# Half slots that gather at their head, without a drain of GpSimd: fused attention and expert layers on one core

## The chip, the cores and the metric

The kernel runs on one core of a Trainium2 chip. The metric is the device time of one execution in microseconds (us). The kernel before took 798.23 us, the median of three runs (797.21 to 799.9).

## What is computed

The reference has two parts. The first is attention over 8 sequences of 448 tokens with 12 heads of 64, with a sigmoid in place of a softmax. The second sends each of the 3584 tokens (768 values) to one of 8 experts:

```python
attn = 1.0 / (1.0 + np.exp(-scores)); attn_out = np.matmul(attn, v)
logits = x @ w_gate
e_idx = np.argmax(logits, axis=1)
for e in range(E):
    mask = e_idx == e
    h = np.maximum(x[mask] @ w1[e], 0.0)
    ye = h @ w2[e]
    out[mask] = gate_w[mask, None] * eom[mask, e, None] * ye
```

All of it is float32. The tokens of an expert are known only on the chip, after the gates.

## The kernel before, in words

Attention comes first. Its rows go to a table in device memory (`x_dram`), and a list of tokens for each expert is built beside it. Then the expert layers run in slots. A slot is a group of tokens of one expert: 256 in a full slot (`slot`, L622), 192 in a wide slot (`wide_slot`, L669), 128 in a half slot (`half_slot`, L693). The number of each kind depends on the data, so `build` (L901) writes the full slots that always exist as straight code and wraps every further slot in an `If` on a count read from the chip (L970, L975, L980). With these inputs three wide slots and two half slots run; the other six half slots, like the other five wide slots, are skipped. The two half slots are the last work of the kernel.

Every product of a slot is made with operands split in a high and a low float32r part: ScalarE (ACT) makes the high part, VectorE (DVE) the low part (`split`, L534; `split_w1_row`, L548; `low_w1`, L541). TensorE (PE) multiplies the tokens by w1 (in a half slot L720 to L722), ACT applies the ReLU, PE transposes the result (`turn`, L702) and multiplies it by w2 (`layer2_mm`, L597). `layer2_out` (L613) scales the two halves of an output row on ACT (L616) and, behind the second, GpSimd (POOL) writes 128 rows to the output with one indirect DMA (L618).

A slot also prepares the next one. SP loads the next slot's weights (`load_slot`, L518; `load_w2`, L530). POOL gathers rows of `x_dram` into the one buffer `xg` with one indirect DMA for each group of 32 tokens times four parts (`gather`, L501, issued at L504): four DMAs for a half slot. DVE turns `xg` over (`turn_x`, L558, at L561), and the result is split for the next slot.

The order on each engine is the order of the program: nothing is moved by a scheduler. In a half slot j of the kernel before it is, on POOL: from the second half slot on a `drain()` of the engine (L699); after `turn_x` of half slot j + 1 the gathers for half slot j + 2 (L736), which need `xg` to be free; then the output DMA of half slot j (L618). The last wide slot gathers for two half slots ahead, so that half slot 0 finds in `xg` the tokens of half slot 1. The lists and the weight tables have entries for all eight half slots. Where a half slot does not exist, its list points to filler rows; its gathers, its `turn_x` and its splits are still issued by the slot ahead of it, and the weights of it are not transferred.

```python
if j:
    nc.gpsimd.drain()
...
self.turn_x(nx)
if j + 2 < E:
    self.gather(self.half_lists(j + 2))
```

`slot` has one more drain of POOL, in the last full slot that is written as straight code (L638). At the end of the program the framework itself issues drains on every engine and a barrier of all engines (they carry line L1016). On the path of a skipped `If` each engine makes up for the semaphore counts of the code left out; on POOL one of these is the instruction INC_SWDGE_SEM (L973 for the wide slots, L978 for the half slots).

Of the kernel before, what the change touches and what calls it, by code (L numbers as in the profile page):

```python
# [22 lines left out]
E = 8  # L23
# [31 lines left out]
def r32(ap):  # L55
    return ap.bitcast(F32)


class Kernel:
# [633 lines left out]
    def half_slot(self, j, y):  # L693
        nc = self.nc
        nx = None
        if j + 1 < E:
            nx = self.load_slot(self.tab_b, j + 1, self.half_lists(j + 1))
        if j:
            nc.gpsimd.drain()  # L699
        (wh, wl), (xh, xl), (hh, hl) = self.w1s, self.xs, self.hs  # L700

        def turn(n):  # L702
            ps = self.take("x", self.psx).rearrange("p a (b t) -> p (a b) t", b=2)
            for i in range(4):
                nc.tensor.transpose(ps[:, i], self.hb[:, 128 * (4 * n + i):128 * (4 * n + i + 1)], self.ident)
            fs = slice(4 * n, 4 * n + 4)
            self.split(ps, hh[:, fs, 0:HS], hl[:, fs, 0:HS])

        w2 = [self.w2_rows(k) for k in range(4)]
        low = lambda k: nc.vector.tensor_tensor(w2[k][2], w2[k][0], r32(w2[k][1]), ALU.subtract)  # L710
        for n in range(2):
            c = slice(512 * n, 512 * n + 512)
            ps = self.take("h", self.psh)
            for d in range(6):
                if n == 1 and d == 3:
                    turn(0)
                    low(2)
                    nc.scalar.copy(w2[3][1], w2[3][0])
                    low(3)
                nc.tensor.matmul(ps, xh[:, d, 0:HS], wh[d][:, c], start=(d == 0), stop=False)  # L720
                nc.tensor.matmul(ps, xh[:, d, 0:HS], wl[d][:, c], start=False, stop=False)
                nc.tensor.matmul(ps, xl[:, d, 0:HS], wh[d][:, c], start=False, stop=(d == 5))  # L722
            if n == 0:
                self.split_w2(0)
                self.split_w2(1)
            nc.scalar.activation(self.hb[:, c], ps, AF.Relu)
            if n == 0:
                nc.scalar.copy(w2[2][1], w2[2][0])
        cur = dict(lt=self.ltb[:, j])
        pss = [self.take("y", self.psy)[:, 0:384] for n in range(2)]  # L730
        self.layer2_mm(pss[0], 0, 0, range(2))
        turn(1)
        if nx is not None:
            self.turn_x(nx)
            if j + 2 < E:
                self.gather(self.half_lists(j + 2))  # L736
            self.split_w1(0)
            for k in range(3):
                self.split_x(nx, k)
            self.split_w1(1)  # L740
        self.layer2_mm(pss[0], 0, 0, range(2, 4))
        self.layer2_mm(pss[1], 0, 1, range(4))
        self.load_w2(nx)
        if nx is not None:
            self.split_w1_row(4)
        for n in range(2):
            self.layer2_mm(pss[n], 0, n, range(4, 8))
            self.layer2_out(pss[n], cur, 0, n, y)
        if nx is not None:
            self.split_w1_row(5)  # L750
# [269 lines left out]
```

## Time and profile before

| what | before |
|---|---|
| median of three runs | 798.23 us (797.21 to 799.9) |
| the profiled execution | 799.36 us |
| its span, first to last instruction | 797.6 us |
| PE busy | 771.8 us, 97% |
| DVE busy | 498.2 us, 62% |
| ACT busy | 490.0 us, 61% |
| POOL busy | 330.4 us, 41%, 468 instructions |
| software DMA queue (POOL's) | 10016 packets, 24.85 MB |
| hardware DMA queue (SP's) | 27696 packets, 119.56 MB |

The span is the time that the trace covers; 1.76 us of the profiled execution lie outside it. Busy times do not count sequencer instructions such as drains, branches and semaphore operations. Those appear in the views with a q behind the engine's name (POOLq). A line in such a view can be that of a helper. A row of the timeline gives the start in us, the duration in us, the engine, the line, the operation, what is written from what, and the idle time ahead of it.

### The profile page before, as it was taken

What the parts mean: (1) busy time and instruction counts of PE and PEld (TensorE: products, weight loads), DVE (VectorE), ACT (ScalarE), POOL (GpSimd) and SP (SyncE); (2) the same over time, 40 slices, a digit from 0 to 9 for tenths busy, and PEclk for the clock granted to TensorE, in tenths of its full rate; (3) what the DMA queues carried; (4) which work ended last, traced back from release to release, by engine and by line L of the source; (5) the groups of instructions that cost most, each with busy time, mean ns of one, the idle gap of its engine ahead of it and who ended that gap; (6) DMA issues with size and microseconds to landing.
All of it is one profiled execution on the core that took longest, in us unless ns stands there. A gap on an engine that the chain in (4) does not pass through costs nothing. (4 is left out here: it accounts for less than half of the span.)

```text
span 797.6 us, 15037 instructions
## 1 busy us (share of the span) xinstructions
PE 771.8 (97%) x5724; PEld 564.3 (71%) x5724; DVE 498.2 (62%) x779; ACT 490.0 (61%) x662; POOL 330.4 (41%) x468
## 2 busy tenths in 40 slices
PE   9999999999999999899999999999999998999893
PEld 4333433333333379799899999999999997888773
DVE  3344435434456668977685775857758575787685
ACT  5666666666668556465574565745657464667674
POOL 4003302320333475657836626345162551543453
PEclk9999999999999999999999999999999999999997
DMA  6353453425458350247468776521165835956861
GB/s 255 133 209 123 163 203 140 180 100 209 150 168 344 110 179 6 80 147 240 184 232 295 236 252 243 169 68 31 50 236 174 299 114 204 349 219 237 288 239 44
DMA packets 37807, 145.61 MB, mean 183 GB/s; under 512 B 5703, under 2 KB 7919, under 8 KB 33744
## 3 DMA queue, kind: packets, MB, share of 16 engines
q1 hardware_dynamic: 27696, 119.56, 42.3%
q0 software_dynamic: 10016, 24.85, 9.4%
q8 instruction: 51, 0.84, 0.4%
q14 instruction: 44, 0.36, 0.2%
HBM read 153.00 MB, written 23.05 MB: 221 GB/s over the span
## 5 line engine op out<-in xcount | busy, mean ns | idle before, releaser
L579 PE MATMUL ps<-rounded 128*128 128x512 f32 (+1 forms) x672 | 229.3, 390 | 5.1 <-ACTq L968 2.9
L504 POOL DMA_INDIRECT plain<-x_dram,lxs x122 | 170.5, 1398 | 151.0 <-DVE plain L561 109.4
L782 ACT ACTIVATE a<-ps,bias_s 128x896 f32<-128x896 f32 x168 | 169.0, 1007 | 101.7 <-PE ps L780 95.2
L580 PE MATMUL ps<-rounded 128*128 128x256 f32 (+1 forms) x672 | 185.3, 276 | 0.9 <-DVE rounded L542 0.9
L536 DVE TENSOR_TENSOR w2l<-plain,w2h 128x1536 fp32r<-128x1536 f32 x60 | 105.3, 1757 | 96.3 <-ACT w2h L535 63.8
L780 PE MATMUL ps<-kqv 64*64 64x448 f32 x1344 | 159.3, 540 | 1.4 <-issue 0.6
L789 PE MATMUL ps<-a,kqv 64*64 64x448 f32 x1344 | 157.4, 536 | 0.0
L579 PEld LDWEIGHTS ps<-rounded 128*128 128x128 f32 x672 | 127.5, 190 | 29.5 <-ACTq L968 3.2
L604 PE MATMUL ps<-w2h,h 128*128 128x384 f32 x432 | 144.8, 335 | 0.0
L606 PE MATMUL ps<-w2h,h 128*128 128x384 f32 x432 | 144.4, 334 | 0.0
L605 PE MATMUL ps<-w2l,h 128*128 128x384 f32 x432 | 144.3, 334 | 0.0
L580 PEld LDWEIGHTS ps<-rounded 128*128 128x128 f32 x672 | 128.9, 192 | 1.2 <-DVE rounded L542 1.2
L542 DVE TENSOR_TENSOR rounded<-plain,rounded 128x2048 fp32r<-128x2048 f32 x46 | 103.7, 2285 | 6.2 <-ACT rounded L539 4.6
L789 PEld LDWEIGHTS ps<-a,kqv 64*64 64x64 f32 x1344 | 52.3, 133 | 74.5 <-issue 73.3
L780 PEld LDWEIGHTS ps<-kqv 64*64 64x64 f32 x1344 | 49.1, 133 | 75.8 <-issue 63.5
L535 ACT CAST w2h<-plain 128x1536 fp32r<-128x1536 f32 x60 | 88.1, 1472 | 10.6 <-PE ps L819 4.4
L539 ACT CAST rounded<-plain 128x2048 fp32r<-128x2048 f32 x46 | 87.5, 1902 | 0.0
L587 ACT COPY gl<-ps 128x256 f32<-128x256 f32 (+1 forms) x112 | 40.2, 359 | 70.2 <-PE ps L580 59.7
L604 PEld LDWEIGHTS ps<-w2h,h 128*128 128x128 f32 x432 | 81.1, 188 | 2.3 <-issue 1.8
L605 PEld LDWEIGHTS ps<-w2l,h 128*128 128x128 f32 x432 | 81.1, 188 | 0.1
L606 PEld LDWEIGHTS ps<-w2h,h 128*128 128x128 f32 x432 | 81.1, 188 | 0.0
L616 ACT ACTIVATE y<-ps,lts 128x384 f32<-128x384 f32 x50 | 29.0, 580 | 69.3 <-PE ps L606 49.6
(206 smaller groups left out, 691.4 us busy)
## 6 DMA issues: line engine op xcount, KB each, us to landing
plain<-w SPq DMA_DIRECT2D x68, 768.0 KB
plain<-w SPq DMA_DIRECT2D x48, 1024.0 KB
kqv<-kqv SPq DMA_DIRECT2D x23, 1344.0 KB
x_dram<-xt SPq DMA_DIRECT2D x8, 1344.0 KB
plain<-w SPq DMA_DIRECT2D x6, 512.0 KB
plain<-x_dram,lxs POOLq DMA_INDIRECT x122
kqv<-kqv SPq DMA_DIRECT2D x1, 896.0 KB
lst<-plain POOLq DMA_DIRECT2D x1, 726.0 KB
```

Of the source, the lines that this page charges most:

```text
L504: self.nc.gpsimd.indirect_dma_start(out=s["xg"][:, g], out_offset=None, in_=x4, in_offset=bass.IndirectOffsetOnAxis(ap=s["lx"][:, g:g + 1] ...
L535: self.nc.scalar.copy(hi, raw)
L536: self.nc.vector.tensor_tensor(lo, raw, r32(hi), ALU.subtract)
L542: self.nc.vector.tensor_tensor(self.w1p[1][k], self.w1r[:, 2 * k:2 * k + 2], r32(self.w1p[0][k]), ALU.subtract)
L579: nc.tensor.matmul(out, wh[d][:, c], both, start=(d == 0), stop=False)
L580: nc.tensor.matmul(ps[:, 0:n], wl[d][:, c], self.xc[:, d, 0, 0:n], start=False, stop=(d == 5))
L604: nc.tensor.matmul(ps, hh[:, f, tk], wh, start=(f == 0), stop=False)
L605: nc.tensor.matmul(ps, hh[:, f, tk], wl, start=False, stop=False)
L606: nc.tensor.matmul(ps, hl[:, f, tk], wh, start=False, stop=(f == 7))
L780: nc.tensor.matmul(ps[half[h], j, 0:S], kg[half[j], e, 0, o:o + 64], kg[half[j], e, 1], start=True, stop=True)
L782: nc.scalar.activation(at[u % 4], ps[:, :, 0:S], AF.Sigmoid, bias=self.bias_s, scale=1.0 / math.sqrt(D))
L789: nc.tensor.matmul(self.ps_o[e][h][half[j], 0:S], v[half[h], 6 if i == 3 else 3 * e + c, j], a[half[h], j], start=(i in ((0, 3 if h else 4 ...
```

## The change

From the second half slot on, a half slot issues the gathers for the next half slot as its first work on POOL. The gathers behind `turn_x` are gone, and so is the drain. Half slot 0 gathers nothing.

```diff
         if j + 1 < E:
             nx = self.load_slot(self.tab_b, j + 1, self.half_lists(j + 1))
-        if j:
-            nc.gpsimd.drain()
+        if nx is not None and j:
+            self.gather(self.half_lists(j + 1))
         (wh, wl), (xh, xl), (hh, hl) = self.w1s, self.xs, self.hs
...
         turn(1)
         if nx is not None:
             self.turn_x(nx)
-            if j + 2 < E:
-                self.gather(self.half_lists(j + 2))
             self.split_w1(0)
             for k in range(3):
                 self.split_x(nx, k)
```

## Rows read from the trace of the kernel before

**Rows 1.** Chain that ended last, from 785 us on: start us, us, what.
```profile
790.91 0.95 POOL plain L504
```

**Rows 2.** Timeline of POOL, half slots 0 and 1.
```profile
767.04 2.91 POOL L504 DMA_INDIRECT plain<-x_dram,gl  x1 [0.30 <-issue]
...
772.49 1.36 POOL L504 DMA_INDIRECT plain<-x_dram,gl  x1 [0.30 <-issue]
774.15 1.41 POOL L618 DMA_INDIRECT out<-y,gl  x1 [0.30 <-issue]
785.34 1.76 POOL L504 DMA_INDIRECT plain<-x_dram,gl  x1 [9.77 <-issue]
...
792.16 1.00 POOL L618 DMA_INDIRECT out<-y,gl  x1 [0.30 <-issue]
```

**Rows 3.** Timeline of ACT, the last output scalings of half slots 0 and 1.
```profile
767.48 1.03 ACT L616 ACTIVATE y<-ps,gl 128x384 f32<-128x384 f32 x2
...
785.56 0.58 ACT L616 ACTIVATE y<-ps,gl 128x384 f32<-128x384 f32 x1 [0.33 <-PE ps L606]
```

**Rows 4.** Drains of POOL by line: durations in ns (min/median/max), first and last start.
```profile
L638 POOLq DRAIN  x1: 7182/7182/7182, 411.8 to 411.8; - x1
...
L699 POOLq DRAIN  x1: 15910/15910/15910, 768.6 to 768.6; - x1
...
L1016 POOLq DRAIN  x1: 537/537/537, 796.3 to 796.3; - x1
...
L1016 POOLq DRAIN  x1: 109/109/109, 797.0 to 797.0; - x1
```

**Rows 5.** Stretches: us, PE, PEld, DVE, ACT, POOL busy (xinstructions), PEclk, DMA share, GB/s.
```profile
411.90:775.70 363.80, 356.82 (x2079) 328.70 (x2078) 255.16 (x318) 225.87 (x329) 162.00 (x109) 1.00 0.58 203
775.70:797.60 21.90, 9.83 (x57) 9.32 (x55) 12.83 (x12) 9.79 (x12) 6.60 (x5) 0.77 0.19 58
...
776.00:777.50 1.50, 1.50 (x10) 1.37 (x9) 1.50 (x2) 1.32 (x2) 0.00 (x0) 1.00 0.67 261
777.50:784.50 7.00, 7.00 (x44) 6.99 (x43) 7.00 (x9) 5.93 (x7) 0.00 (x0) 1.00 0.02 5
```

**Rows 6.** DMA issues on POOL's queue, 0 to 411.9 us.
```profile
lst<-plain POOLq DMA_DIRECT2D x1, 726.0 KB
plain<-x_dram,lxs POOLq DMA_INDIRECT x40
lst<-meta,posi POOLq DMA_INDIRECT x32
...
out<-y,lts POOLq DMA_INDIRECT x6
hb<-lst,gl POOLq DMA_INDIRECT x5
wg<-wgo POOLq DMA_DIRECT2D x1, 48.0 KB
...
lists<-lst,gl POOLq DMA_INDIRECT x2
```

**Rows 7.** Timeline of DVE, half slots 0 and 1.
```profile
766.80 2.29 DVE L542 TENSOR_TENSOR rounded<-plain,rounded 128x2048 fp32r<-128x2048 f32 x1
...
771.27 3.42 DVE L536 TENSOR_TENSOR w2l<-plain,w2h 128x1536 fp32r<-128x1536 f32 x2
...
779.91 0.97 DVE L561 STREAM_TRANSPOSE plain<-plain 128x768 f32<-128x768 f32 x1
...
786.18 2.35 DVE L536 TENSOR_TENSOR rounded<-plain,rounded 128x1024 fp32r<-128x1024 f32 x2
```

**Rows 8.** POOL's sequencer where the skipped slots end: durations in ns, first and last start.
```profile
L973 POOLq INC_SWDGE_SEM  x1: 2253/2253/2253, 760.1 to 760.1; - x1
...
L978 POOLq EVENT_SEMAPHORE  x4: 17/43/43, 795.2 to 795.5; - x4
...
L978 POOLq INC_SWDGE_SEM  x1: 278/278/278, 795.6 to 795.6; - x1
```

## The prediction

> **What bounds the kernel now.** I read the chain of waits first, then POOL's timeline, then the rows of the drains. TensorE is busy for 97% of the span, but not at the end. The chain that ended last runs in its last stretch through POOL alone: it passes through a gather at 790.91 us [rows 1] that fetches filler rows for a half slot that does not exist. The output of half slot 1 was ready long before: ACT finished the scaling at 785.56 + 0.58 = 786.14 us [rows 3], but the output DMA, last in POOL's order, was issued from 792.16 to 793.16 us [rows 2]. In front of it stood four gathers, the first from 785.34 us, and in front of those the drain of L699. That drain was reached at 768.6 us and took 15.91 us, until 784.5 us [rows 4]; POOL's last instruction ahead of it, the output DMA of half slot 0, ended at 774.15 + 1.41 = 775.56 us [rows 2]. So for 8.95 us the drain alone kept POOL. Behind the last output DMA come its landing (POOL's sequencer goes on at 795.2 us, 2.04 us after the issue [rows 8]), the make-up of semaphores, the drains of the program's end and a barrier, up to 797.6 us.
>
> What does a drain wait for? Not for data: the 392 KB of the output DMA of half slot 0 (261 GB/s over 1.5 us) are through by 777.5 us, and from there to 784.5 us the DMA engines carry 5 GB/s [rows 5], with no POOL instruction. The three drains that have work behind them line up with something else, the number of DMAs that POOL has issued since the drain before. Up to the drain of L638 these are 40 + 32 + 6 + 5 + 2 + 1 + 1 = 87 [rows 6], and it takes 7.18 us [rows 4]: 82.5 ns each. Between it and L699 every POOL instruction is a DMA, 109 of them [rows 5], and the drain takes 8.95 us after the last: 82.1 ns each. From there to the end there are five [rows 5], and the first drain of the program's end takes 0.537 us, against 0.109 us for the one after it with none left [rows 4]: 86 ns each. I read this as bookkeeping of the ring, some 82 ns for each DMA that has not been accounted for, done when a drain asks for it.
>
> **The change, part by part.**
>
> *The gathers behind turn_x and at the head.* In half slot 0 four gathers go, so its output DMA no longer stands behind them. Its scaling ends at 767.48 + 1.03 = 768.51 us [rows 3]. A POOL DMA that meets a DVE subtraction of two SBUF tensors ends about 0.87 us after that subtraction: the gather of 767.04 ended at 769.95 us and DVE's operation at 769.09 us; the gather of 772.49 ended at 773.85 us and the first of DVE's pair at 771.27 + 1.71 = 772.98 us [rows 2, 7]. So the output DMA ends at about 769.96 us. Half slot 1's four gathers follow at once; `xg` is free, since half slot 0's turn_x lies ahead of all this. They take the places that the trace has from 769.95 to 772.2, 772.49 to 773.85 and 774.15 to 775.5 us, and one from 775.85 us, that ends at 776.9 us if it meets no DVE operation and at 778.6 us if it meets a whole one of 1.71 us. The output DMA's data were down by 1.94 us after its issue ended [rows 5], with four times a gather's bytes; at most that much more makes 780.5 us for the last gather.
>
> *Who waits for them now.* DVE's turn_x in half slot 1 started at 779.91 us [rows 7], so it may come 0 to 0.6 us later. Behind it on DVE and ACT stand splits for a slot that does not exist, and the last scaling; ACT idled 0.33 us ahead of that one [rows 3]. I take 0 and keep +0.3 us. PE waits for none of it: turn_x comes after the last operand of half slot 1. SP's queue carries no weights then.
>
> *The last output DMA.* Nothing stands in front of it any more: drain and gathers are gone, POOL is free from 778.6 us at the latest. It is ready at 786.14 us and meets DVE's pair of 786.18 us, 2.35 us for two [rows 7]: the first ends at 787.36, the DMA at 788.2 us. If it met neither it would end at 787.2, if both at 789.4 us. Against 793.16 us this is **-5.0 us** (-6.0 to -3.8).
>
> *The drain.* L699 is taken away with its 8.95 us of work, which stood ahead of gathers that nobody used; that gain is inside the -5.0 us and not counted again. But the 109 DMAs that it accounted for are still there when the program's end drains POOL, with the last output DMA 110 (four gathers fewer in half slot 0, four as before in half slot 1, counting from L638). At 82.2 ns that drain takes 9.0 us instead of 0.54 us: **+8.5 us**. Nothing covers it: in the trace it begins at 796.3 us, 1.1 us after the landing, with all other engines done, and the barrier waits for it. If the work starts only after landing, 109 DMAs take 784.5 - 777.5 = 7.0 us, and the term is +6.5 us. If a drain's time does not depend on what is outstanding, it is 0. I take +8.5 us, since three drains of 5, 87 and 109 DMAs lie on one line through it.
>
> *The make-up of semaphores.* INC_SWDGE_SEM on the skipped path took 2.25 us at 760.1 us and 0.28 us at 795.6 us [rows 8]. The first stood behind some hundred DMAs not yet drained, the second behind five; but the first was also the first of its kind and ran under weight loads. If the ring is the reason, this one costs 2.0 us more now. I take 0, from the row at the same place, and keep +2.0 us.
>
> **Sum:** -5.0 + 8.5 + 0 + 0 = +3.5 us. The profiled execution (799.36 us for a span of 797.6) would become 802.9 us; it stood 1.1 us above the median of 798.23 us, so the forecast for the median is 801.8 us, 0.4% slower. With all ends of the terms it runs from -6.0 + 6.5 = +0.5 to -3.8 + 0.3 + 8.5 + 2.0 = +7.0 us: 798.7 to 805.2 us. About 0.3%, or 2.4 us, is what a measurement of this kernel can tell from no change.
>
> **The rivals.**
>
> *The drain's time does not come back (faster).* The mechanism is in the last drain of the program: if it stays near 0.54 us, only the -5.0 us is left: 793.2 us. For it speaks that a drain written by the kernel need not do the same as the one of the framework; against it, that the latter took five times the 0.109 us of its successor with just five DMAs to account for [rows 4]. It decides from the point where the last drain is under 0.54 + 5.0 = 5.5 us. The Trainium skill, in "VectorE: DVE Perf Modes", section "The DRAIN you can't avoid", says that the drains of a program's preamble and postamble are about 12 ns on all five engines, constant: by that rule this rival wins, with 793.2 us. POOL's 537 and 109 ns do not agree with it.
>
> *Half of it comes back (no change).* POOL is idle from about 778.6 to 786.1 us, and if a part of the bookkeeping is done there without being asked, or while the last DMA lands, some 4.3 us remain: -0.7 us, 797.5 us. Against it: between the two drains POOL was busy for only 162 of 363.8 us [rows 5], and L699 still shows 82 ns for each of 109.
>
> *The gathers land late (slower still).* Turn_x then holds the last scaling, one for one beyond 0.33 us. With quiet queues from 768 us on there is little to make them late; a delay of 5 us beside the forecast would give 806.8 us.
>
> **How the numbers follow.** The forecast has 0.74, the faster rival 0.15, the half 0.07, late gathers 0.04. The ends of the terms leave some 0.10 of the forecast's chance under +2.4 us. So: slower by over 0.3% 0.64 + 0.04 = 0.68; within 0.3% 0.10 + 0.06 = 0.16; faster 0.15 + 0.01 = 0.16. The range takes the forecast and the half, from 797.5 to 805.5 us, and leaves out the faster rival and late gathers, about 0.2. The likeliest case's own range is 798.7 to 805.2 us.
>
> **What would show it.** In the changed kernel's profile the output DMA of half slot 0 should be issued at about 769 us and four gathers right behind it; turn_x of half slot 1 should start at 779.9 to 780.5 us; the last output DMA should end at about 788.2 us, and POOL's sequencer pass L978 at about 790.3 us. Then the first drain of the program's end should take about 9 us instead of 0.54 us and be the last item of the chain. If that drain is short, the forecast is wrong and the faster rival holds; if INC_SWDGE_SEM shows 2 us, the sum was 2 us too low; if turn_x starts after 781 us, the gathers were late.

## The result, and the profile after

The changed kernel took 806.56 us (median of four runs, 806.43 to 808.18) against 798.03 us (with a fourth run of the kernel before): a ratio of 1.0108, 95% interval 1.0086 to 1.013. It is slower by 8.5 us, where 3.5 us had been forecast, and it lies 1.1 us above the range. The profiled execution took 808.18 us with a span of 806.5 us.

POOL's timeline in the two half slots (start us, us, engine, line, operation, idle time ahead) answers to [rows 2]:

```profile
771.78 1.14 POOL L618 DMA_INDIRECT out<-y,gl  x1 [15.43 <-ACT y L616]
773.23 1.98 POOL L504 DMA_INDIRECT plain<-x_dram,gl  x1 [0.30 <-DVE rounded L536]
...
778.81 0.95 POOL L504 DMA_INDIRECT plain<-x_dram,gl  x1 [0.30 <-issue]
789.37 1.86 POOL L618 DMA_INDIRECT out<-y,gl  x1 [9.61 <-ACT y L616]
```

The four gathers follow the output DMA of half slot 0 at once, and the last output DMA waits for nothing but ACT's scaling. These rows of DVE and ACT, half slot 1, answer to [rows 3, 7]:

```profile
782.87 0.97 DVE L561 STREAM_TRANSPOSE plain<-plain 128x768 f32<-128x768 f32 x1
...
788.51 0.58 ACT L616 ACTIVATE y<-ps,gl 128x384 f32<-128x384 f32 x1 [0.32 <-PE ps L606]
```

Turn_x does not wait for the gathers. But the scaling ends at 789.09 us, 2.95 us later than before: all of this stretch, both half slots, is late. Measured from the end of the scaling, the last output DMA ends after 2.14 us (791.23 us) against 7.02 us before. That is the gain, 4.9 us. What follows it is lost again. These are the sequencer rows of POOL where skipped code ends (L966 the full slots, L971 the wide, L976 the half slots) and at the end of the program, to be read against [rows 4, 8]; durations in ns:

```profile
L966 POOLq INC_SWDGE_SEM  x1: 1790/1790/1790, 675.4 to 675.4; - x1
...
L971 POOLq INC_SWDGE_SEM  x1: 2253/2253/2253, 763.1 to 763.1; - x1
...
L976 POOLq INC_SWDGE_SEM  x1: 2373/2373/2373, 793.7 to 793.7; - x1
...
L1014 POOLq DRAIN  x1: 9039/9039/9039, 796.3 to 796.3; - x1
```

The last drain takes 9.04 us in place of 0.54 us, and INC_SWDGE_SEM 2.37 us in place of 0.28 us. With the same landing time (2.47 against 2.44 us from the end of the issue to INC_SWDGE_SEM) the end of the program changes by -4.9 + 2.1 + 8.5 = +5.7 us. The other 2.9 us arose far ahead of the half slots. 0.6 us of them are there before 30 us (a copy of DVE to `xh` starts at 29.95 us against 29.34 us). The routing's reciprocal at L299, still attention, stands at 277.46 us against 275.15 us, 2.3 us late. Stretches of the changed kernel (us, then PE, PEld, DVE, ACT, POOL busy, PEclk, DMA share, GB/s):

```profile
262.00:266.00 4.00, 2.80 (x9) 0.61 (x10) 2.25 (x4) 1.01 (x1) 3.26 (x11) 1.00 0.27 80
266.00:268.00 2.00, 1.51 (x9) 0.92 (x12) 1.17 (x2) 1.01 (x1) 0.91 (x7) 0.65 0.00 0
268.00:270.00 2.00, 2.00 (x16) 1.26 (x12) 0.22 (x2) 1.01 (x1) 0.00 (x0) 0.50 0.00 0
```

and of the kernel before:

```profile
262.00:266.00 4.00, 2.75 (x14) 0.63 (x11) 1.67 (x3) 1.01 (x1) 3.52 (x14) 1.00 0.27 74
266.00:268.00 2.00, 2.00 (x23) 1.40 (x26) 1.53 (x3) 1.90 (x2) 0.32 (x2) 1.00 0.00 0
268.00:270.00 2.00, 2.00 (x22) 0.96 (x17) 1.12 (x4) 1.03 (x2) 0.00 (x0) 1.00 0.33 35
```

In both, PE is idle for some 1.2 of the 4 us from 262 to 266 us; in the changed kernel TensorE's granted clock then fell to 0.50 (1.2 GHz) until 270 us, in the kernel before it stayed at 1.00 (2.4 GHz). A second such stretch lies at the head of the first wide slot. Its rows, that of the kernel before ahead of the changed one's:

```profile
661.30:664.70 3.40, 3.40 (x13) 3.40 (x14) 1.40 (x1) 1.49 (x2) 0.54 (x1) 0.50 0.96 303
662.50:669.40 6.90, 6.24 (x23) 6.24 (x24) 2.11 (x2) 1.80 (x2) 1.33 (x2) 0.51 0.90 317
```

Here both kernels ran at the lower clock, the changed one twice as long. ACT's cast at 650.50 us is 2.2 us late, its copy at 675.86 us 3.3 us. So the lateness of this execution grew by 1.7 us at the first fall of the clock and by 1.1 us at the second; by the half slots a little of it was made up again. Whether the change has a part in this was a question for the runs.

### The profile page after: what moved, and what is told of

Read it like the earlier page. It is cut to its first block, busy times and chain, and to the rows that moved or that the text cites. A ratio compares the mean times of both kernels' runs of the same rounds, so it can differ in the third digit from the quotient of the medians.

```text
span 806.5 us, 15030 instructions
## 1 busy us (share of the span) xinstructions
PE 775.1 (96%) x5724; PEld 566.5 (70%) x5724; DVE 498.3 (62%) x779; ACT 491.0 (61%) x662; POOL 327.6 (41%) x464
## 3 DMA queue, kind: packets, MB, share of 16 engines
q0 software_dynamic: 9824, 24.46, 9.0%
## 5 line engine op out<-in xcount | busy, mean ns | idle before, releaser
L504 POOL DMA_INDIRECT plain<-x_dram,lxs x122 | 172.3, 1412 | 142.9 <-DVE plain L561 99.1
```

The lines of the kernel that those rows point to most:

```text
L504: self.nc.gpsimd.indirect_dma_start(out=s["xg"][:, g], out_offset=None, in_=x4, in_offset=bass.IndirectOffsetOnAxis(ap=s["lx"][:, g:g + 1] ...
```

## The experiments

The runs came from several chips; the kernel before took 794 to 800 us on them, so each is given as a ratio to the kernel before on its own chip. The times are medians; a ratio is estimated from all runs and can differ a little from the quotient of the two medians. "Number 114" is the 114th DMA that POOL issued since the drain of L638, and "accounts" is my word for the bookkeeping of DMAs that a drain has yet to do.

### The drain behind the gathers

```diff
         if nx is not None and j:
             self.gather(self.half_lists(j + 1))
+            nc.gpsimd.drain()
```

> The changed kernel with the drain put back into half slot 1, behind the four gathers instead of ahead of them. Theory (a drain, and INC_SWDGE_SEM too, pays for every DMA that POOL issued since the last drain): the drain begins when the fourth gather is issued, takes 109 x 82 ns = 8.9 us, and is over just before the last scaling is ready, so it costs nothing. The first drain of the program's end then has one DMA left and takes about 0.2 us, INC_SWDGE_SEM about 0.3 us. Time: the changed kernel less 8.8 less 2.1 us, 795.6 us; if the 2.8 us by which the changed kernel came late already ahead of the half slots go as well, 793 us. Rival (the last drain is long because of where it stands, or its length has nothing to do with the count): the drain in half slot 1 or the one at the end does not follow the count, the last one stays near 9 us, time 806 us. Rival for INC_SWDGE_SEM (long the first time or under weight loads, not for the count): 0.3 us cannot be told apart here, see the run with drains in the wide slots.

Measured: 789.93 us against 795.12 us, a ratio of 0.9941 (0.992 to 0.9961). The drain, the last drain and the last INC_SWDGE_SEM:

```profile
L700 POOLq DRAIN  x1: 15043/15043/15043, 766.1 to 766.1; - x1
...
L1015 POOLq DRAIN  x1: 212/212/212, 786.9 to 786.9; - x1
...
L977 POOLq INC_SWDGE_SEM  x1: 198/198/198, 786.2 to 786.2; - x1
```

The fourth gather ended at 772.19 us and the drain at 781.14 us: 8.95 us for 109 DMAs, as in the kernel before. The output DMA behind it was issued at 782.07 us, 0.5 us after the end of the scaling at 781.54 us, so the drain is covered. One line decides the sign of the change: with a drain behind them the gathers at the head are worth 0.6%, and the drain's absence costs more than that.

### Only the drain taken out

```diff
-        if j:
-            nc.gpsimd.drain()
```

> The kernel before with only the drain of half slot 1 taken out; the gathers stay behind turn_x. Theory: POOL's four gathers in half slot 1 start when turn_x is through, at about 781 us, and the last output DMA ends some 3 to 4 us earlier than the 793.2 us of before; then the last drain takes 114 x 82 ns = 9.4 us and INC_SWDGE_SEM about 2.3 us: 798.0 - 3.5 + 8.9 + 2.1 = 805.5 us, up to 808 us with the late start seen in the changed kernel. Rival (it is the gathers at the head that lengthen the end): the last drain stays at 0.5 us and the time is 794.5 us.

Measured: 793.85 us, a ratio of 0.9992 (0.9977 to 1.0007): no difference that can be told. The theory failed. The last drain came out short, as the rival has it, but the 3.5 us that both had counted on did not come: the gathers, the first at 773.78 us, kept POOL until 783.23 us. The last output DMA, POOL's INC_SWDGE_SEM and the last drain:

```profile
783.53 1.00 POOL L618 DMA_INDIRECT out<-y,gl  x1 [0.30 <-issue]
...
L976 POOLq INC_SWDGE_SEM  x1: 337/337/337, 786.9 to 786.9; - x1
...
L1014 POOLq DRAIN  x1: 703/703/703, 787.5 to 787.5; - x1
```

No drain stands between L638 and the end, 114 DMAs were issued, and yet the last drain is short. The scaling ended at 778.78 us, so the output DMA ended 5.75 us behind it, 1.3 us better than before; the two short items cost 0.2 us more. The 0.703 us are those of about seven outstanding DMAs on the scale of the other rows. So either something had cleared all but some seven of the accounts on the way, in this kernel and not in the changed one, which issues 110, or it matters where the gathers lie (the rival). The runs with more gathers test that.

### Drains in the wide slots

```diff
         self.layer2(cur, 0, 1, self.ys[0])
+        self.nc.gpsimd.drain()
```

(at the end of `wide_slot`; the half slots as changed)

> The changed kernel with a drain at the end of each wide slot, none in the half slots. Theory (both instructions go by the count): the three drains take about 85 x 82 ns = 7 us, then 8 DMAs each, 0.7 us, all while POOL has nothing else to do; INC_SWDGE_SEM behind the wide slots falls from 2.25 to about 0.3 us, so turn_x of half slot 0 starts up to 2 us earlier and PE's wait in half slot 1 shrinks; the last drain has 6 DMAs and takes 0.6 us, the last INC_SWDGE_SEM about 0.3 us. Time: 806.6 - 8.4 - 2.0 - 1.5 = 794.7 us. Rival for INC_SWDGE_SEM (first of its kind, or weight loads on the DMA engines): the one behind the wide slots stays at 2.25 us, and the time is 796.2 us.

Measured: 790.03 us, a ratio of 0.994 (0.9919 to 0.9962). The drains in the wide slots, INC_SWDGE_SEM behind the wide slots and the drains at the end:

```profile
L692 POOLq DRAIN  x3: 4490/8438/8477, 694.4 to 747.0; - x3
...
L972 POOLq INC_SWDGE_SEM  x1: 173/173/173, 756.3 to 756.3; - x1
...
L1015 POOLq DRAIN  x3: 46/109/632, 785.5 to 786.7; - x3
```

INC_SWDGE_SEM right behind a drain takes 0.17 us where it took 2.25 us, under the same weight loads: it goes by the count of undrained DMAs, as the drain does. The first of the three drains has 88 DMAs and ends 7.25 us after the last issue, as the count has it. The two later ones had eight DMAs and still took 4.5 and 8.4 us. Each stood behind an output DMA, with the weights of the next slot on the DMA engines, and these two output DMAs (issued at 723.83 and 747.26 us) landed late, 3.9 and 7.8 us after their start:

```profile
out<-y,lts POOLq DMA_INDIRECT x1, 3.9
out<-y,lts POOLq DMA_INDIRECT x1, 7.8
```

That is at 727.7 and 755.1 us; the drains ended 0.4 us later, at 728.1 and 755.5 us. Three drains of five or eight DMAs in the kernel with both kinds of drain (below) also ended 0.3 to 0.4 us after a landing. So I read a drain as lasting until the accounts are done and the last data have landed, whichever comes later. The prediction's "Not for data" holds for its three drains, whose data were down first, and not in general. No run changed the landing alone.

### Thirty small DMAs

```diff
         o = 6 * DF * 4
+        small = c(0, 30, 16, dt=F32, parts=1)
+        for i in range(30):
+            self.nc.gpsimd.dma_start(small[:, i], self.wgo[i:i + 1, 0])
```

(in `memory`; the half slots as changed)

> The changed kernel with 30 further DMAs of 64 bytes on POOL's queue, ahead of the drain of L638; the output stays the same. Theory (the count of DMAs): the drain of L638 has 117 in place of 87 and takes 117 x 82.5 ns = 9.6 us. Rival (packets or bytes): 30 to 480 packets more on 3744, 0.1% of the bytes more: 7.2 to 8.1 us. The last drain stays at 9.0 us, the time within 0.3% of the changed kernel, since nobody waits for the drain of L638.

Measured: 800.41 us in one run, beside a median of 795.12 us for the kernel before. The drain of L638 (L641 here):

```profile
L641 POOLq DRAIN  x1: 9629/9629/9629, 410.3 to 410.3; - x1
```

9.63 us for 117 DMAs against 7.18 us for 87: 30 DMAs of 64 bytes cost 2.45 us, 82 ns each, as much as a gather of 96 KB or an output DMA of 384 KB. The count is what is paid for, not packets or bytes. The small DMAs made more packets than the expectation allowed for, 960 (10784 in place of 9824 on POOL's queue), but packets do not order the drains: these 117 DMAs made 4784 of them, and the 109 of the kernel before, whose drain is shorter, 5920. The last drain stayed at 9.03 us.

### More gathers

```diff
         if nx is not None and j:
             self.gather(self.half_lists(j + 1))
+            self.gather(dict(lx=self.lxb[:, j + 1], xg=self.xg[:, 4:8]), groups=range(4))
```

> The changed kernel with four further gathers of filler rows in half slot 1, into a part of the buffer that nobody reads. They stand behind the four gathers, while POOL has nothing else to do. Counted from the drain of L638 the last output DMA is number 114 in place of 110. In the kernel before without its drain, number 114 came and the last drain took 0.70 us with no drain ahead of it. Theory (the ring has room for the rows of fewer than 114 such DMAs, and when it is full the accounts are cleared on the way at no visible cost): the last drain takes 0.7 us, INC_SWDGE_SEM 0.34 us, and more work makes the kernel 8.3 + 2.0 us faster than the changed kernel, some 0.6% faster than the kernel before. Rival (it was the gathers behind turn_x, or the four gathers in half slot 0, that kept the end short there): the last drain takes 114 x 82 ns = 9.4 us and INC_SWDGE_SEM 2.5 us, time as the changed kernel or 0.5 us more.

Measured: 790.84 us against 793.96 us, a ratio of 0.9962 (0.9946 to 0.9977): four useless gathers make the changed kernel faster than the kernel before.

```profile
776.84 2.11 POOL L504 DMA_INDIRECT plain<-x_dram,gl  x1 [0.30 <-issue]
782.96 1.51 POOL L618 DMA_INDIRECT out<-y,gl  x1 [4.01 <-ACT rounded L535]
...
L977 POOLq INC_SWDGE_SEM  x1: 338/338/338, 786.9 to 786.9; - x1
...
L1015 POOLq DRAIN  x1: 703/703/703, 787.4 to 787.4; - x1
```

The last drain has the same 0.703 us as in the kernel with the drain taken out, whose gathers lie elsewhere. So the rival, the place of the gathers, falls. The output DMA, number 114, started 1.7 us after its scaling ended at 781.22 us, where the changed kernel has 0.3 us; if this is the clearing, it costs at most 1.5 us. In the kernel with only the drain taken out no DMA near number 114 has more than the usual 0.30 us of idle time ahead of it, so nothing of the clearing is seen there.

With two further gathers (the same line with `range(2)`):

> The same with two further gathers: the last output DMA is number 112. Theory: if the ring is full only at 113 or 114, the last drain takes 112 x 81 + 130 ns = 9.2 us and INC_SWDGE_SEM 2.5 us, time as the changed kernel; if it is full at 111 or 112, the drain takes 0.5 to 0.7 us, some 10 us less. Rival (the place of the gathers): as the changed kernel in either case.

Measured: 798.42 us in one run. The last INC_SWDGE_SEM and the drains at the end:

```profile
L977 POOLq INC_SWDGE_SEM  x1: 2413/2413/2413, 783.7 to 783.7; - x1
...
L1015 POOLq DRAIN  x3: 46/109/9197, 786.6 to 796.4; - x3
```

112 DMAs are not cleared, 114 are. The threshold of these runs lies between, with DMAs of 128 rows; with 30 small ones among them 117 went by without clearing, so it is not the bare number of DMAs that decides. Where the count starts is open: the two kernels that were cleared issue 201 DMAs from the program's start, this one 199, and no run tells a count from the start from one since the last drain.

### The drain ahead of the gathers

```diff
         if nx is not None and j:
+            nc.gpsimd.drain()
             self.gather(self.half_lists(j + 1))
```

> The changed kernel with the drain put back at its old place, ahead of the gathers, which stay at the head of half slot 1. Theory (a drain holds POOL for 82 ns per DMA, and whoever needs what is queued behind it waits): it accounts for 105 DMAs, 8.6 us from the end of half slot 0's output DMA; the four gathers follow, and turn_x of half slot 1 waits for them 5 to 6 us; the last scaling and the last output DMA are late by as much; the last drain (5 DMAs) 0.5 us and INC_SWDGE_SEM 0.3 us are short again. Time within 1 us of the kernel before: what the drain's absence saves at the end is what turn_x loses. Rival (the gathers' place hardly matters, only whether there is a drain): turn_x does not wait, as in the run with the drain behind the gathers, 0.6% faster than before.

Measured: 800.39 us against 799.71 us, a ratio of 1.0013 (0.9992 to 1.0033): no difference that can be told. The drain, and turn_x of half slot 1:

```profile
L699 POOLq DRAIN  x1: 9950/9950/9950, 765.5 to 765.5; - x1
...
783.14 0.98 DVE L561 STREAM_TRANSPOSE plain<-plain 128x768 f32<-128x768 f32 x1 [6.27 <-DMA plain<-x_dram,gl]
```

From the end of the output DMA (766.80 us) the drain takes 8.65 us for 105 DMAs, and turn_x waits 6.27 us. One line lower, on another chip, the drain was free.

### The changed kernel again, on two other chips

No edit.

> The changed kernel itself, timed again beside the other runs. What the change does to the end of the program is worth -4.9 + 2.1 + 8.5 = +5.7 us by its own profile; in the first comparison it came out 8.5 us slower, because everything from 264 us on was late by 2.3 to 3.4 us. Theory (that lateness is a dip of TensorE's granted clock near 266 us that happened in those runs and has nothing to do with the change): here +5.7 us, 0.7% slower than the kernel before. Rival (the change brings the dip with it, by the place of its code or of its queues): +8.5 us, 1.1% slower, with a granted clock under 0.9 between 262 and 272 us.

Measured: 800.35 us against 793.96 us, a ratio of 1.0074 (1.0057 to 1.009), +5.9 us by the ratio. And once more:

> The changed kernel a third time, on whatever chip comes. The first comparison gave +8.5 us (before 798.0 us), the second +5.9 us (before 794.0 us). Theory: the end of the program gives +5.7 us, and what was above it was a dip of TensorE's clock near 266 us, on a chip where PE waits there. On a chip with before at 798 us or more: between +5.7 and +8.5 us, and the more the lower the granted clock between 262 and 272 us; on a chip with before near 794 us: +5.7 us. Rival (the change has a cost of its own of 2.8 us ahead of the half slots): +8.5 us whatever the clock shows there.

Measured: 801.2 us against 794.96 us, a ratio of 1.0075 (1.0056 to 1.0095), +6.0 us by the ratio. The stretch from 262 to 272 us in the first of these:

```profile
262.00:272.00 10.00, 10.00 (x105) 4.00 (x100) 6.56 (x15) 5.50 (x10) 5.13 (x17) 1.00 0.39 123
```

and the last drain, with 9.03 us in both. PE does not wait there and the granted clock stays at 1.00. The 5.7 us of the end lie in both intervals and the 8.5 us in neither, so the further 2.8 us do not belong to the change wherever it runs. Why they were in all four runs of the first chip, on which the kernel before took 798 us, stays open: neither repetition came to such a chip, and of the four runs one has a trace.

### Both kinds of drain

The drain behind the gathers and the one at the end of each wide slot together, on two chips.

> The changed kernel with a drain at the end of each wide slot and one behind the gathers of half slot 1. Theory: nothing is left for the end. INC_SWDGE_SEM about 0.2 us behind the wide slots and at the end, the last drain 0.2 us: 0.5 us better than with the wide slots' drains alone, 1 to 2 us better than with the half slot's alone (turn_x of half slot 0 waits no more for INC_SWDGE_SEM), 0.7 to 0.8% faster than the kernel before. Rival (the time of the end is set by PE and DVE by now, not by POOL): the same as the two runs with one kind of drain, 0.6% faster.

Measured: 788.41 us, a ratio of 0.9928 (0.9908 to 0.9948). Behind the wide slots, at the end, and turn_x's wait in half slot 0:

```profile
L973 POOLq INC_SWDGE_SEM  x1: 173/173/173, 754.9 to 754.9; - x1
...
L1016 POOLq DRAIN  x3: 46/109/128, 783.9 to 785.0; - x3
...
DVE plain L561 <- DMA plain<-x_dram,lxs: 1.9, 1, 1.9
```

> The changed kernel with drains at the end of each wide slot and behind the gathers of half slot 1, a second time. Theory: 0.7% faster than the kernel before, as on the other chip (0.9928). Rival: on a chip where the kernel before takes longer, what comes ahead of the end gives the gain back, 0.3% or less.

Measured: 788.11 us against 794.96 us, a ratio of 0.9906 (0.9885 to 0.9927). This is the fastest kernel of the study, faster than both the kernel before and the changed one. But turn_x of half slot 0 still waited 1.9 us in the first and 2.3 us in the second run for data to land. Without drains in the wide slots this wait took 1.2 to 4.9 us, and with them alone 0.5 us, so the expected gain there was not shown; whether both kinds of drain are better than one cannot be told from these intervals.

## Why the prediction fell short

*What bounds the end* was read rightly: POOL's queue, with gathers that nobody uses in front of the last output. The 2.95 us of lateness taken off, the fourth gather ended at 776.8 us (forecast 776.9 to 778.6), turn_x started at 779.9 us (779.91), and the last output DMA ended at 788.3 us (788.2). The term of -5.0 us measured -4.9 us.

*The drain*, +8.5 us, measured +8.5 us: 9.04 us for 110 DMAs. Of the drains of the study, these, taken from the end of the last issue, lie on one line of 0.13 us + 81 ns for each DMA:

| DMAs since the last drain | 1 | 5 | 6 | 87 | 105 | 109 | 110 | 112 | 117 |
|---|---|---|---|---|---|---|---|---|---|
| drain, us | 0.21 | 0.54 | 0.63 | 7.18 | 8.65 | 8.95 | 9.04 | 9.20 | 9.63 |

The drains that wait for landing do not fit, nor do two more. The last drain of the kernel with both kinds took 0.13 us with one DMA outstanding. That of L638 in the first profile of the changed kernel ended 9.2 us after the last issue for 87 DMAs. Its cause was not sought.

*The faster rival* falls: the framework's drain at the end pays the same price as one in the kernel. By the rule of the Trainium skill weighed there ("VectorE: DVE Perf Modes", section "The DRAIN you can't avoid") it should have been about 12 ns; 9.04 us was measured, and the measurement decides.

*The make-up of semaphores* is the step that failed. The forecast said "I take 0, from the row at the same place, and keep +2.0 us"; it measured +2.1 us, beyond the end that had been kept. The wrong choice was to hold the 2.25 us at 760.1 us for a first call or an effect of weight loads. The trace of before had a row that excludes the first call (the weight loads are excluded by the 2.37 us at the changed kernel's end, where the DMA share is 0.00), and I did not read it:

```profile
L968 POOLq INC_SWDGE_SEM  x1: 1801/1801/1801, 673.3 to 673.3; - x1
```

That was an earlier one, behind 80 undrained DMAs. With 104 (2.25 us) and 5 (0.28 us) it lies on a line of 0.17 us + 20 ns for each DMA, and so do the 2.37 us behind 110, the 2.41 us behind 112 and the 0.17 us right behind a drain. With it the sum would have been +5.6 us, or 803.9 us, and two other chips gave +5.9 and +6.0 us. On the first chip this miss alone would have left the time inside the range.

*What no step had:* the 2.8 us ahead of the half slots on the first chip. The prediction took all that lies ahead of the half slots as unchanged, without a term for it. In the one trace of that chip these stretches gave 1.7 us at the fall of the clock at 266 us and 1.1 us at the longer one at 662 us. They put the result above the range, and they were not the change's on the other two chips; their cause stays open.

*The ring that clears itself* was not in the forecast either. It does not touch this result, since 110 DMAs were not cleared, but the forecast's rule that the 109 DMAs "are still there" holds, in these kernels, only up to some number between 112 and 114 DMAs of 128 rows.

## What to carry to other kernels

Count the DMAs that GpSimd has issued since its last drain: here each costs 81 ns in the next drain and 20 ns in INC_SWDGE_SEM, and a program that never drains on the way pays at its end, where nothing covers it. A drain belongs behind the last thing that somebody waits for and ahead of an idle stretch of POOL as long as the drain: moved one line down it went from no gain that can be told to 0.6% faster, on two chips. When a row could be explained in several ways, look for its further occurrences in the same trace before choosing the cheap one.

## What the runs showed of the hardware that I had not expected

Somewhere between 112 and 114 DMAs of 128 rows all but some seven of the ring's accounts are cleared without a drain (I read it as the ring being full; no run shows its size or from where it counts): with 114 DMAs of 128 rows the last drain took 0.70 us, with 112 it took 9.20 us, and the clearing, if the late output DMA is its cost, took at most 1.5 us against the 9 us of a drain. So four superfluous gathers saved some 9 us. And INC_SWDGE_SEM, which only makes up counts for skipped code, takes up to 2.4 us by the same count. And a drain with few DMAs outstanding can still be long: with eight it took up to 8.4 us until the last of them had landed.
